# Weight loads and k's block loads issued by GpSimd instead of SyncE, in attention followed by an MLP

## The chip, the cores and the metric

The kernel runs on one core of a Trainium2 chip. The metric is the device time of one execution in microseconds (us); the time before is the median of three runs, 882.17 us (881.49 to 883.12). The core has a matrix engine (TensorE, PE in the profile), three engines for elementwise work (VectorE or DVE, ScalarE or ACT, GpSimd or POOL), and SyncE (SP), which only issues transfers. Each engine works through its own list of instructions in order, and semaphores order them against each other. An engine that reaches an instruction whose semaphore is not there yet stands still, with everything behind it in its list. Transfers between the main memory (HBM) and the on-chip memory (SBUF) run on 16 DMA engines; SP, ACT and POOL can issue them.

## What is computed

The reference has two parts. The first is attention over 4 batches of 8 heads with 768 positions of 64 numbers, in which a query sees only those keys whose hash bucket is equal to its own. The second is an MLP with a learned negative slope on the attention's output.

```python
q_bits = (np.einsum('bhsd,dk->bhsk', q, proj) > 0)      # 6 bits a position; k alike
mask = q_bucket[:, :, :, None] == k_bucket[:, :, None, :]
scores = np.where(mask, scale * np.matmul(q, k.transpose(0, 1, 3, 2)), -1e9)
attn = softmax(scores)                                  # with 1e-9 in the divisor
x = np.matmul(attn, v)  # then (B,H,S,D) -> (B*S, H*D) = 3072 x 512
h = x @ w_in                                            # 512 x 2048
g = np.maximum(h, 0.0) + alpha * np.minimum(h, 0.0)
out = g @ w_out                                         # 2048 x 512
```

q, k, v and proj are float32. The two weight matrices arrive as float64.

## The kernel before

There are two stages. In the first, a loop over 16 pairs of heads does the attention, and beside it the weights are converted. In the second the MLP runs with products of the Strassen kind, so that sums and differences of weight blocks are needed; they are made beside the attention too, and kept in HBM.

The 16 pairs are worked on one after the other (the loop at line 1168). For a pair, PE makes 12 cells of scores (`scores`, lines 760 to 771: two matmuls on hash bits and two on q and k for each cell, into one of three buffers `sc` in PSUM). ACT takes the exponential of each cell into `pt` (L771). PE multiplies with v (`attend`, L801, into `av`). DVE adds the exponentials up (L779 to L790), PE sums these over the partitions (`totals`, L815), and DVE turns and inverts the sums (`divide`, L831 to L834). In the next pair, POOL copies the reciprocals between groups of 32 partitions (L840, L841), DVE spreads them (L843) and multiplies `av` by them (L849), and SP stores the result `x` (L850). The hash bits of the next pair come from PE (L730) and ACT (L736), and POOL's DMAs put them into place (L741, L743): six small transfers a pair, behind ACT's L736.

q and k come in by blocks of 32 x 32 (`load_blocks`, lines 505 to 515): four DMAs for a tensor and pair, each of 32 partitions by 24 runs of 32 numbers. DVE turns the blocks (`turn_blocks`, L704), k's at the start of the pair ahead. ACT takes the largest squares (`magnitude`, L711), after which the buffer is free; there are three buffers for each of q and k, and before the change both are refilled at the end of the pair, for the third pair ahead (lines 1221 to 1224). v has its own load (L488).

The weights come in 32 pieces of 128 x 512 float64 numbers, two a pair (`load_weight`, lines 578 to 582, three buffers `raw`). A piece is converted in steps: ACT reads it (`weight_abs`, L596 and L600), DVE clamps, shifts and joins (L606, L612, L637, L640); L637 is the last to read `raw`, and L640 the last to read ACT's output, which has two buffers. Piece i + 3 is asked for right after the last step of piece i. POOL makes the sums of four pieces (`weight_sums`, L676 and L659), one in front of the reciprocal copies and one before that in most pairs, and SP stores them (L651, L664). From pair 9 on, SP also loads x back and the first weights of the second stage (L864, L880).

The compute instructions are wrapped in `do`, which keeps them in the order of the program. The DMAs are not: a scheduler places them in their engine's list, and each also waits until the DMA eight before it of its kind (those issued by SP and ACT, or those issued by POOL) has landed, since there are eight semaphores for each kind.

Of the kernel before, what the change touches and what calls it, by code (L numbers as in the profile page):

```python
# [407 lines left out]
def fast_path(  # L408
# [12 lines left out]
    nc = tc.nc  # L421
# [33 lines left out]
    NPAIR = len(pairs)  # L455
# [27 lines left out]
    def load(pi, name):  # L483
        b, hp = pairs[pi]
        src = {"q": q, "k": k, "v": v}[name]
        if name == "v":
            t = pool.tile([P, 2, NC * D], F32, name=f"vn{pi}", tag="vn")
            nc.sync.dma_start(t, src[b, 2 * hp : 2 * hp + 2].rearrange("h (p c) d -> p h (c d)", c=NC))  # L488
            nat[name, pi] = t
        elif pi and name in BY_BLOCKS:  # L490
            load_blocks(pi, name)
        else:
            load_part(pi, name, slice(0, NC), nc.sync)

    def load_part(pi, name, cs, queue):
        b, hp = pairs[pi]
        src = {"q": q, "k": k}[name]
        if cs.start == 0:
            nat[name, pi] = pool.tile([P, NC, 2, D], F32, name=f"{name}n{pi}", tag=f"{name}n", bufs=3)
        for s in range(2):  # L500
            queue.dma_start(nat[name, pi][:, cs, s], src[b, 2 * hp + s].rearrange("(p c) d -> p c d", c=NC)[:, cs])

    BY_BLOCKS = 'qk'

    def load_blocks(pi, name):
        b, hp = pairs[pi]
        src = {"q": q, "k": k}[name]
        nat[name, pi] = t = pool.tile([P, NC * 4, 32], F32, name=f"{name}n{pi}", tag=f"{name}n", bufs=3)
        for s in range(2):
            for h in range(2):  # L510
                a = D * s + 32 * h
                nc.sync.dma_start(
                    t[a : a + 32].rearrange("i (c u) d -> i c u d", u=4),
                    src[b, 2 * hp + s, :, 32 * h : 32 * h + 32].rearrange("(u i c) d -> i c u d", u=4, c=NC),
                )
# [39 lines left out]
    raw, wx, wr = {}, {}, {}  # L555
# [3 lines left out]
    def piece(i):  # L559


        if i < HW:
            n, m = divmod(i, 4)
            c, kk = divmod(n, 2)
            o, j = kk + 2 * (m // 2), c + 2 * (m % 2)
            return moe_w_in[o * P : (o + 1) * P, j * 512 : (j + 1) * 512]
        n, m = divmod(i - HW, 2)
        o = n + NI * m
        return moe_w_out[o * P : (o + 1) * P]
# [5 lines left out]
        ahead = (i + 1) * HW // TURNS > HW - len(left[0])  # L575
        order.append(left[0 if left[0] and ahead or not left[1] else 1].pop(0))

    def load_weight(i):
        if i < NW:
            i = order[i]  # L580
            raw[i] = pool.tile([P, 512], moe_w_in.dtype, name=f"raw{i}", tag="raw", bufs=3)
            nc.sync.dma_start(raw[i], piece(i))

    def halves(i):
        words = raw[i].bitcast(U32).rearrange("p (f t) -> p f t", t=2)
# [16 lines left out]
    def weight_clamp(i):  # L602
        if i < NW:
            i = order[i]
            x = wx[i]
            do(DVE.tensor_scalar(x, x, HI_MIN, None, op0=ALU.max, op1=ALU.max, accum_out=wmax[:, i : i + 1]))  # L606
# [76 lines left out]
    def two_banks(name):  # L683
        return psum.tile([P, 2, 512], F32, name=name, tag="sc", bufs=3)
# [17 lines left out]
    def turn_blocks(pi, name):  # L702
        tr[name, pi] = pool.tile([P, S], F32, name=f"{name}T{pi}", tag=f"{name}T")
        do(DVE.transpose(tr[name, pi], nat[name, pi].rearrange("p w d -> p (w d)")))  # L704
# [8 lines left out]
    def hash_bits(pi, halves=BOTH, engine=None):  # L713

        if halves.start == 0:
            bits["q", pi] = qbs[pi % 2]
            kb = pool.tile([P, 3 * CW], BF16, name=f"kb{pi}", tag="kb", bufs=1)
            bits["k", pi] = kb[:, :S]  # L720
            bits["raw", pi] = kb.rearrange("p (a w) -> p a w", w=CW)
        ps = {"k": two_banks(f"hs{pi}")}
        ps["q"] = psum_av.tile([P, 2, 512], F32, name=f"hsq{pi}", tag="av") if engine is DVE else ps["k"]
        for half in range(halves.start, halves.stop):
            for name in "qk" if engine is DVE else "kq":
                for s in range(2):
                    r, c = D * s, D * (s ^ half) + 32 * "kq".index(name)

                    for t, c in [("k", c)] + ([("q", c ^ D)] if engine is DVE and name == "q" else []):
                        do(PE.matmul(  # L730
                            ps[t][c : c + 32, half if t == "k" or engine is not DVE else 0, :CW], wh[r : r + D],
                            tr[name, pi][r : r + D, half * CW : (half + 1) * CW], start=True, stop=True,
                        ))
        if engine is None:
            raw = bits["raw", pi]
            do(ACT.activation(raw[:, 0:3:2], ps["k"][:, :, :CW], AF.Sign, bias=hb))  # L736
            for half in range(2):
                for s in range(2):
                    c = D * (s ^ half)
                    cols = slice(half * CW, (half + 1) * CW)  # L740
                    nc.gpsimd.dma_start(bits["q", pi][D * s : D * s + 32, cols], raw[c + 32 : c + 64, 2 * half])  # L741
                    if half:
                        nc.gpsimd.dma_start(bits["k", pi][D * s : D * s + D, cols], raw[c : c + D, 2])  # L743
            return
        for half in range(halves.start, halves.stop):
            cols = slice(half * CW, (half + 1) * CW)
            for s in range(2):
                c = D * (s ^ half ^ (engine is DVE)) + 32
                do(ACT.activation(
                    bits["q", pi][D * s : D * s + 32, cols], ps["q"][c : c + 32, 0 if engine is DVE else half, :CW], AF.Sign, bias=hb[c : c + 32],  # L750
                ))

            for to, c, n in [(0, 0, P)] if half == 0 else [(0, D, D), (D, 0, D)]:
                dst, src = bits["k", pi][to : to + n, cols], ps["k"][c : c + n, half, :CW]
                do(DVE.tensor_scalar(
                    dst, src, hb_k[c : c + n, 0:1], hb_k[c : c + n, 1:2], op0=ALU.is_gt, op1=ALU.subtract,
                ))
# [19 lines left out]
    def add_first(pi):  # L777
        accp[pi] = pool.tile([P, 2 * NCH, CW], F32, name=f"accp{pi}", tag="accp", bufs=1)
        do(DVE.tensor_tensor(accp[pi], p(0), p(1), op=ALU.add))  # L779
# [362 lines left out]
    for half in (first, second):  # L1142
        turn(0, "q", half)
        turn(0, "k", half, DVE)
        if half is first:
            nil[0]()
            hash_bits(0, first, DVE)
    load(1, "q")
    load(1, "k")
    load_weight(0)  # L1150
    load(0, "v")
    for i in range(1, 3):
        load_weight(i)
# [14 lines left out]
    for pi in range(NPAIR):  # L1168
        i = 2 * pi

        def weight_begin():
            if pi + 1 < NPAIR:
                turn_blocks(pi + 1, "k")
            weight_clamp(i)
            weight_parts(i)
            add_first(pi)

        scores(pi, [c for c in CELLS if pi or c not in ahead])
        if pi:
            divide(pi - 1, weight_begin)  # L1180
        else:
            add_first(pi)
        weight_sum(i)
        weight_group(i)
        load_weight(i + 3)
        if pi == 0:
            weight_abs(1, DVE)
        weight_clamp(i + 1)
        add_third(pi)
        add_last(pi)  # L1190
        add_total(pi)
        weight_parts(i + 1)
        weight_sums(1, weight_sum(i + 1))
        weight_group(i + 1)
        load_weight(i + 4)
        if pi + 1 < NPAIR:
            hash_bits(pi + 1)
            do(ACT.activation(tr["q", pi + 1], tr["q", pi + 1], AF.Copy, scale=DOWN))
        if pi + 2 < NPAIR:
            turn_blocks(pi + 2, "q")  # L1200
        attend(pi)
        if pi + 1 == NPAIR:
            now = ff1(0, 0)
            now.step(1)
        totals(pi)
        if pi + 1 == NPAIR:
            now.step(5)
            divide(pi)
        else:
            weight_abs(i + 2)  # L1210
        if pi + 2 < NPAIR:
            load(pi + 2, "v")
        if pi in (9, 11, 15):
            load_w((9, 11, 15).index(pi))
        if pi in (9, 10, 12):
            load_x(0, *{9: (0,), 10: (2, 3), 12: (1,)}[pi])
        if 11 <= pi < 14 or pi == 15:
            sum_x(0, min(pi - 11, 3), DVE)
        if pi == 1:
            setup_alpha()  # L1220
        for name in "qk":
            magnitude(pi, name)
            if pi + 3 < NPAIR:
                load(pi + 3, name)
        if pi + 1 < NPAIR:
            weight_abs(i + 3)
# [97 lines left out]
```

## Time and profile before

The profile is of one execution. Its own time is 882.06 us; the span, from the first instruction to the last, is 880.2 us.

| | before |
|---|---|
| median of three runs | 882.17 us |
| profiled execution, and its span | 882.06 us, 880.2 us |
| PE busy | 863.0 us (98%) |
| DVE busy | 749.2 us (85%) |
| ACT busy | 368.0 us (42%) |
| POOL busy | 96.8 us (11%) |
| DMAs issued by SP and ACT (queues 1 and 10) | 124.8 MB |
| DMAs issued by POOL (queue 0) | 11.3 MB |
| one pair in the steady state | 19.15 us |
| a k load on SP, of four a pair | 660 ns median to issue, 3.6 us from issue to landing |
| a weight piece on SP | 337 to 364 ns to issue, 4.5 to 4.9 us to landing |
| a bit transfer on POOL (L741) | 505 ns, 3.6 us to landing |
| a 512 KB load on POOL (L989, second stage) | 759 ns, 7.2 us to landing |

How to read it: a row of the groups or the timeline gives engine, line, operation, output tile and input tiles, and in square brackets the idle time before it with what ended it. Rows with a q behind the engine (SPq) are issues of DMAs, whose time is that of issuing and not of moving the data. In the windows, each engine's busy time is followed by the granted PE clock (1.00 is full), the busy share of the DMA engines and GB/s.

### The profile page before, as it was taken

How to read it: one execution, taken by the hardware profiler on the slowest of the kernel's cores; microseconds unless marked ns; L12 is line 12 of the kernel's file. 1: busy time of each engine (PE TensorE's matmuls, PEld its weight loads, DVE VectorE, ACT ScalarE, POOL GpSimd, SP SyncE). 2: the span in 40 equal slices, each digit the busy share in tenths (PEclk: the TensorE clock that was granted, in tenths of full speed). 3: DMA queues.
4: the chain of work that ended last, by engine and by line, in shares of the span. 5: the costliest groups of instructions: out<-in, count | busy, mean ns of one | idle time of the engine just before them, and what ended most of it. 6: DMA issues, size and time to landing. Idle time of an engine off the chain costs nothing.

```text
span 880.2 us, 15210 instructions
## 1 busy us (share of the span) xinstructions
PE 863.0 (98%) x5706; PEld 576.0 (65%) x5706; DVE 749.2 (85%) x1215; ACT 368.0 (42%) x654; POOL 96.8 (11%) x220
## 2 busy tenths in 40 slices
PE   8999999999998999999999999999999999999996
PEld 3444444444443445559996558996557997557996
DVE  5999999999997978899888769898668988668986
ACT  6886888887766752221112222112222112222111
POOL 1221423323322311120000000000000000000000
PEclk9999999999998999999999999999999999999998
DMA  8866797797796347586433425334434333520242
GB/s 197 183 152 136 181 241 157 169 253 192 177 252 169 118 150 263 203 303 223 133 132 90 172 86 197 115 113 125 141 123 155 136 123 96 177 86 1 96 151 69
DMA packets 170819, 137.23 MB, mean 156 GB/s; under 512 B 126016, under 2 KB 154384, under 8 KB 167152
## 3 DMA queue, kind: packets, MB, share of 16 engines
q1 hardware_dynamic: 163136, 123.64, 49.5%
q0 software_dynamic: 5184, 11.34, 3.9%
q10 hardware_dynamic: 2416, 1.18, 0.5%
q8 instruction: 47, 0.77, 0.4%
q14 instruction: 36, 0.29, 0.1%
HBM read 104.87 MB, written 28.31 MB: 151 GB/s over the span
## 4 chain that ended last, share of the span: by engine, by line
PE 92%; DVE 3%; DMA 2%; issue 1%; ACT 1%; SPq 1%; ACTq 0%; DVEq 0%
PE sc L768 15%; PE av L801 13%; PE f_0a L902 2%; PE z_4a L902 2%; PE z_7a L902 2%; PE z_3a L902 2%; PE z_6a L902 2%; PE z_5a L902 2%; PE z_1a L902 2%; PE z_2a L902 2%; PE f_4a L902 2%; PE f_7a L902 2%; PE f_6a L902 2%; PE f_5a L902 2%; PE f_3a L902 2%; PE f_2a L902 2%
## 5 line engine op out<-in xcount | busy, mean ns | idle before, releaser
L771 ACT ACTIVATE pt<-sc 128x768 f32<-128x768 f32 x192 | 154.0, 812 | 8.3 <-PE sc L768 6.8
L768 PE MATMUL sc<-qT,kT 64*128 64x384 f32 x768 | 157.3, 488 | 0.0
L801 PE MATMUL av<-pt,vn 128*32 128x385 f32 (+1 forms) x1536 | 127.4, 486 | 0.0
L801 PEld LDWEIGHTS av<-pt,vn 128*32 128x32 f32 x1536 | 48.7, 109 | 77.5 <-issue 69.3
L768 PEld LDWEIGHTS sc<-qT,kT 64*128 64x128 f32 x768 | 69.3, 190 | 38.4 <-issue 38.1
L768 PE MATMUL sc<-qb,kb 64*128 64x384 bf16 x384 | 63.8, 328 | 8.0 <-ACT pt L771 7.0
L955 DVE TENSOR_TENSOR g<-g,g 128x384 f32<-128x384 f32 x128 | 68.3, 554 | 2.2
L1019 DVE TENSOR_TENSOR gs<-g,gs 128x768 f32<-128x768 f32 x56 | 53.3, 951 | 1.0
L1011 DVE TENSOR_TENSOR ws<-wl 128x512 f32<-128x512 f32 x56 | 38.4, 686 | 18.2 <-DMA wl<-w_out_s 16.3
L1019 DVE TENSOR_TENSOR gs<-g 128x768 f32<-128x768 f32 x56 | 53.2, 951 | 0.0
L596 ACT ACTIVATE wr<-raw 128x512 int32<-128x512 uint32 x32 | 22.1, 692 | 59.1 <-issue 30.2
L741 POOL DMA_DIRECT2D qb<-kb x60 | 30.1, 505 | 146.3 <-ACT kb L736 146.3
L768 PEld LDWEIGHTS <-kb 64*128 64x128 bf16 x384 | 19.6, 95 | 38.7 <-issue 14.1
L779 DVE TENSOR_TENSOR accp<-pt,pt 128x1536 f32<-128x1536 f32 x16 | 28.2, 1760 | 17.9 <-ACT pt L771 17.9
L951 DVE SCALAR_TENSOR_TENSOR g<-h,alpha 128x384 f32<-128x384 f32 x32 | 19.7, 616 | 25.2 <-ACT h L944 25.1
L784 DVE TENSOR_TENSOR accd<-accd,pt 128x1536 f32<-128x1536 f32 x16 | 28.1, 1758 | 1.7
L790 DVE TENSOR_TENSOR accd<-accd,accp 128x1536 f32<-128x1536 f32 x16 | 28.1, 1758 | 0.6
L787 DVE TENSOR_TENSOR accp<-accp,pt 128x1536 f32<-128x1536 f32 x16 | 28.0, 1753 | 0.0
L783 DVE TENSOR_TENSOR accd<-pt,pt 128x1536 f32<-128x1536 f32 x16 | 28.0, 1750 | 0.0
L902 PE MATMUL f_0a<-x,wi 128*128 128x384 f32 x64 | 23.5, 489 | 0.0
L902 PE MATMUL f_1a<-x,wi 128*128 128x384 f32 x64 | 23.3, 486 | 0.0
L902 PE MATMUL f_2a<-x,wi 128*128 128x384 f32 x64 | 23.3, 486 | 0.0
(355 smaller groups left out, 1740.2 us busy)
## 6 DMA issues: line engine op xcount, KB each, us to landing
wi<-w_in_s SPq DMA_DIRECT2D x32, 896.0 KB, 4.7
wl<-w_out_s SPq DMA_DIRECT2D x16, 1024.0 KB, 4.8
wl<-w_out_r SPq DMA_DIRECT2D x12, 1024.0 KB, 5.0
raw<-in_moe_w_out_dram SPq DMA_DIRECT2D x16, 512.0 KB, 4.9
raw<-in_moe_w_in_dram SPq DMA_DIRECT2D x16, 512.0 KB, 4.5
w_in_s<-wsi SPq DMA_DIRECT2D x16, 448.0 KB, 5.7
qn<-in_q_dram SPq DMA_DIRECT2D x64, 96.0 KB, 5.4
vn<-in_v_dram SPq DMA_DIRECT2D x16, 384.0 KB, 5.6
```

The lines of the kernel that those rows point to most:

```text
L741: nc.gpsimd.dma_start(bits["q", pi][D * s : D * s + 32, cols], raw[c + 32 : c + 64, 2 * half])
L768: do(PE.matmul(sc[:, s, :CW], what["k", pi][r, ks], what["q", pi][r, qs], start=first, stop=not first,))
L771: do(ACT.activation(pts[kc][:, g, :, :CW], sc[:, :, :CW], AF.Exp, scale=SCALE / DOWN))
L779: do(DVE.tensor_tensor(accp[pi], p(0), p(1), op=ALU.add))
L783: do(DVE.tensor_tensor(accd[pi], p(3), p(4), op=ALU.add))
L784: do(DVE.tensor_tensor(accd[pi], accd[pi], p(5), op=ALU.add))
L790: do(DVE.tensor_tensor(accd[pi], accd[pi], accp[pi], op=ALU.add))
L801: do(PE.matmul(av[pi][D * s + t : D * s + t + 32, g, :w], nat["v", pi][:, s, kc * D + t : kc * D + t + 32], pts[kc][:, g, s, :w], start=(k ...
L902: do(PE.matmul(self.ps[bank], self.left(left, k), self.right(right, k), start=start and k == 0, stop=k == self.nk - 1, skip_group_check=no ...
L955: do(DVE.tensor_tensor(new_g(b, to)[:, i], g_m[b, x][:, i], g_m[b, y][:, i], op=ALU.subtract))
L1011: do(DVE.tensor_tensor(t, w2[b, n, x], w2[b, n, y], op=op))
L1019: do(DVE.tensor_tensor(t, g2[b, n, x], g2[b, n, y], op=ALU.subtract))
```

## The change

Three things are moved; nothing that is computed is altered.

- `load_weight` issues its DMA on POOL instead of SP. Piece 0 stays on SP and is asked for ahead of q and k of pair 1, instead of behind them.
- `load_blocks` issues k's four DMAs on POOL for pairs 3 and up. q stays on SP.
- From pair 3 on, k is asked for one pair later: in the program no longer at the end of pair pi for pair pi + 3, but inside pair pi, after `divide(pi - 1)`, for pair pi + 2.

In the lists of instructions that the scheduler makes, PE's, DVE's and ACT's compute instructions stand in the same order as before. POOL's list gets 83 more DMAs (52 of k, 31 of the weights). In a steady pair it reads: piece i + 4; the sum of pieces with its small copy; three of k's four DMAs; the copy that waits for `vs` and, where due, another sum; the four reciprocal copies; k's fourth DMA; piece i + 3 of the next turn; the six bit transfers. So three of the four k loads stand ahead of the reciprocal copies and one behind them, while in the program all four come behind. Pieces 1 and 2 come first of all DMAs in POOL's list, behind the memsets of lines 545 and 547.

```diff
     def load_blocks(pi, name):
+        queue = nc.gpsimd if name == "k" and pi > 2 else nc.sync
...
-                nc.sync.dma_start(
+                queue.dma_start(
...
-    def load_weight(i):
+    def load_weight(i, queue=nc.gpsimd):
         if i < NW:
             i = order[i]
             raw[i] = pool.tile([P, 512], moe_w_in.dtype, name=f"raw{i}", tag="raw", bufs=3)
-            nc.sync.dma_start(raw[i], piece(i))
+            queue.dma_start(raw[i], piece(i))
...
+    load_weight(0, nc.sync)
     load(1, "q")
     load(1, "k")
-    load_weight(0)
     load(0, "v")
     for i in range(1, 3):
         load_weight(i)
...
         if pi:
             divide(pi - 1, weight_begin)
+            if pi + 2 < NPAIR:
+                load(pi + 2, "k")
...
             magnitude(pi, name)
-            if pi + 3 < NPAIR:
+            if pi + 3 < NPAIR and name == "q":
                 load(pi + 3, name)
```

## The prediction

> **What bounds the kernel now.** I read the page first: its busy shares, the slices, the chain. TensorE (PE) is busy for 98% of the span, so an edit of loads can only win where PE stands still, and loses where it makes PE stand.
>
> ```profile
> PE 863.0 (98%) x5706; PEld 576.0 (65%) x5706; DVE 749.2 (85%) x1215; ACT 368.0 (42%) x654; POOL 96.8 (11%) x220
> ```
>
> Then PE's own waits, which name almost all of what it waits for in mid-program, two waits on the exponentials:
>
> ```profile
> PE sc L768 <- ACT pt L771: 7.0, 2, 4.3
> ```
>
> The timeline of PE and ACT puts them at 16.65 (2.68 us) and at 269.11 (4.28 us). Both times ACT stood, in order, in front of a conversion of a weight piece that had not landed. First ACT at the start, then ACT, PE and SP near 260:
>
> ```profile
> 15.23 0.67 ACT L596 ACTIVATE wr<-raw 128x512 int32<-128x512 uint32 x1 [2.68 <-DMA raw<-in_moe_w_out_dram]
> 267.15 0.66 ACT L596 ACTIVATE wr<-raw 128x512 int32<-128x512 uint32 x1 [9.10 <-DMA raw<-in_moe_w_out_dram]
> 269.11 0.51 PE L768 MATMUL sc<-qb,kb 64*128 64x384 bf16 x2 [4.28 <-ACT pt L771]
> 269.38 1.51 PE L768 MATMUL sc<-qT,kT 64*128 64x384 f32 x4
> ```
>
> ```profile
> 247.39 6.25 SPq L512 DMA_DIRECT2D kn<-in_k_dram  x4
> 253.74 4.23 SPq L664 DMA_DIRECT2D w_in_s<-wsi  x4
> 258.07 1.80 SPq L850 DMA_DIRECT2D x_s<-x  x1
> 259.96 2.85 SPq L582 DMA_DIRECT2D raw<-in_moe_w_out_dram  x2
> ```
>
> Read the last four: the piece's buffer is free when DVE's L637, which starts at 250.71 and takes 0.68, has read the old piece, at 251.4. SP was busy with k's loads, stores and x until 259.96, 8.6 us later. PE also pays after the gap: in the windows, the granted clock is 1.00 before 264 and
>
> ```profile
> 269.00:274.50 5.50, 5.39 (x22) 3.14 (x23) 2.65 (x2) 3.39 (x6) 0.00 (x0) 0.51 0.92 129
> ```
>
> **What the Trainium skill says.** "TensorE: Matmul & The Clock Gate", What's actually happening: after an idle window of about 3.4 us the array runs at half clock. The trace agrees: 4.28 us idle, then 0.51. "DMA: Bandwidth & Descriptors", Issuing engines are not separate DMA queues: another issuer saves only sequencer time, the same 16 engines move the data. Here sequencer time is what was lost. "Perfetto Trace Analysis", DMA Instruction — SWDGE (GPSIMD): a GpSimd DMA's row ends when the last descriptor is written; so I take the row as POOL's occupation, and four L989 issues in 3.04 us agree. "SBUF — State Buffer", Who interferes with whom: GpSimd's writing of descriptors and a DVE instruction in a 2-port mode block one another. No row of before shows such an overlap.
>
> **Part 1, the stall near 260.** A piece issued by POOL no longer waits behind SP's 12.6 us of other issues. POOL is free there: its reciprocal copies of this pair end at 246.1. Issue at about 251.4, plus the longest landing seen for a piece, 7.1 us, gives 258.5. (The skill's fit in "DMA: Bandwidth & Descriptors", Anatomy of one DMA, is 2.0 us + bytes/436e3, for 512 KB an estimate of 3.2 us without contention; the trace's median is 4.5 to 4.9.) ACT may start L596 when DVE's L640, at 260.82 for 0.69, frees its buffer: 261.5. So 3 us of margin. PE's fourth cell would follow the third (263.85) by 0.81, at 264.66 instead of 269.11: 4.45 us. The four cells from 269.11 take 5.80 us up to 274.91 instead of 4 x 0.81 = 3.24: 2.56 us. Gain **7.0 us**. The DVE waits of 0.84 and 0.18 (st L831, behind the sums of x) stay.
>
> **Part 2, the start.** Piece 0 moves on SP ahead of q1 and k1: issued at 5.1, not 10.73. It is there when ACT is free for it at 12.55, so ACT could win 2.68 us. But pieces 1 and 2 now go out on POOL as soon as its memsets end, at 2.9. Three pieces of 512 KB are 1.57 MB before k1's blocks are through. The windows give the price:
>
> ```profile
> 4.00:14.00 10.00, 9.53 (x74) 4.57 (x74) 4.12 (x6) 5.81 (x10) 0.00 (x0) 1.00 0.82 153
> 14.00:20.00 6.00, 3.35 (x26) 2.18 (x27) 5.15 (x8) 4.77 (x7) 0.00 (x0) 1.00 1.01 341
> ```
>
> At 341 GB/s they take 4.6 us; the engines had 10 x 0.18 = 1.8 us to spare from 4 to 14; so k1 is about 2.8 us later than the 14.17 at which DVE turned it. The same jam may hold q0's second half (PE waits 0.3 us for it already). DVE has 0.49 us in hand before L779 at 17.34 and works without a gap from there to st L831, which ends at 31.79; PE's third cell of pair 1, whose bank st frees, starts at 32.58, 0.79 later. So 2.8 - 0.49 - 0.79 = 1.5 us lost, with PE's head start at ACT worth nothing, since DVE sets the pace. Lower bound: the mix overlaps freely, k1 is 0.7 us later (one issue of 0.66), and PE gains about 0.6 us. Upper bound: 4.6 - 1.28 = 3.3 us lost. I take **1.0 us lost**.
>
> **Part 3, k's loads on POOL.** POOL's rows: a 32-row bit copy takes 501 ns, a 64-row one 521, an L989 load of 512 runs 753. That is 0.525 ns a run; a k load has 32 x 24 = 768 runs of 128 B, so 0.50 + 736 x 0.525 ns = 0.89 us, four a pair, and about 0.55 for each of two pieces (128 rows): 4.7 us on an engine busy for 3.8 to 6.8 of 19.15 us. What matters is the order. In the scheduled program three of k's four loads stand ahead of the reciprocal copies, between the piece's sums and vs; one behind. In the tightest pairs (two L659 sums around vs; five of them) the copies end at 150.26, and DVE wants them at 152.03, both read off one pair's rows (113.73 + 2 x 19.15 for the DVE one):
>
> ```profile
> 145.89 1.28 POOL L659 TENSOR_TENSOR wsi<-wsi 128x512 f32<-128x512 f32 x1
> 147.73 0.18 POOL L676 COPY late_sum<-vs 128x1 f32<-128x1 f32 x1 [0.56 <-DVE vs L836]
> 150.07 0.19 POOL L841 COPY rr<-rr 32x12 f32<-32x12 f32 x1
> 113.73 0.97 DVE L843 STREAM_TRANSPOSE dn<-rr 128x768 f32<-128x768 f32 x1
> ```
>
> Three loads add 2.67, of which POOL's 0.56 wait for vs hides a part: 2.1 us against 1.77 of slack, 0.3 late. Behind L843 on DVE stand L849 and the sums up to st; st has about 0.6 us in hand before PE's third cell (ends 147.02, cell at 147.62). So nothing reaches PE, until the port adds: L612 (0.43 us where L606 on the same tile takes 0.64, so perhaps such a mode) falls into k's issues and can be held by one, 0.9 us, of which DVE's 0.82 wait before L779 takes most. I charge **0.5 us**; from 0 to 3 (five pairs at 0.6). The waits the pieces bring to POOL (for L637) have only the bit copies behind them, which ACT's kb releases later anyway (138.86 against L637's end at 135.5). The bit copies are queued behind a piece and must land within 4.5 us of the last issue (141.46 to 145.99); the median is 3.1, the maximum 5.1, and pieces preceded them by as much before. Nothing charged; if they slip, it is at most a us in the two or three pairs with w_in_s stores. k is used a pair after its load, some 14 us of cover. SP loses four k issues and two pieces a pair: x and v go out earlier, hidden behind PE.
>
> **The sum.** Against the profiled execution's 882.06 us (span 880.2 plus 1.9 around it), which is 0.11 below the median 882.17: -7.0 + 1.0 + 0.5 = -5.5, so 876.6; on the median's footing **876.7 us**.
>
> **Rivals.** *GpSimd becomes the bound*: if a k load takes more than the line through 32 to 512 rows says, the copies of the five tight pairs are late by 3c - 0.56 - 1.77, less 0.6 of cover. At c = 2 us that is 3.1 each, 15 in all: 892 us. It turns the sign from c = 1.4 us. For it: no row of before has 768 short runs on POOL. Against it: three points lie on one line. Chance 0.13. *The piece is late anyway*: near 260 the DMA share is 0.95 to 1.00, so the data and not the issue could be late; then 7.0 falls away and about 883.5 is left. Against it: the piece landed 7.1 us after its issue even there, and has 10. Chance 0.12. *The start wins too*, on free overlap: 875.1, inside the first case. The forecast, with that, has 0.75.
>
> Changes within 0.2% (1.8 us) are about what a measurement of this kernel can't tell from none. The first case alone runs from 873 (start wins 0.6, POOL free, a little of the DVE waits gone) to 880 (start 3.3, POOL 1). The range takes in the late piece and the beginning of GpSimd's case, to 884. Faster: 0.75 and a little of GpSimd's case, 0.76; same: most of the late piece, 0.09; slower 0.15.
>
> **What would show it** (lines of the kernel before). L596 without a DMA wait near 260 and at 15; PE's waits without the 4.28, clock 1.00 throughout 264 to 280; k rows on POOL near 0.9 us; dn L843 waiting under 0.5 us for rr. In pair 1, DVE's kT near 17 and a PE wait on st. I am wrong if k rows take 1.4 us or more, if dn waits for rr by us in many pairs, or if raw still ends a wait of ACT.

## The result and the profile after

The changed kernel takes **889.96 us** (median of four runs, 889.55 to 890.49), against 882.33 us for the kernel before beside it (881.49 to 883.12): the ratio is 1.0086, with a 95% interval from 1.0071 to 1.0100. It is 0.9% slower, 13 us above the forecast of 876.7 and 6 us above the upper end of the range. The profiled execution is 889.55 us, its span 887.8 us. Lines of the changed kernel are one higher than before from L506 on, and three higher behind the main loop's edit.

The page's shares hardly move for PE. POOL is busy for 172.0 us instead of 96.8, and DVE for 9 us more with the same instructions (5.7 us of it at L613):

```profile
PE 866.0 (98%) x5706; PEld 575.8 (65%) x5706; DVE 758.1 (85%) x1215; ACT 365.7 (41%) x654; POOL 172.0 (19%) x303
```

The view of the waits (engine, tile and line, what it waited for: sum in us, number, longest) tells more. PE's two waits on the exponentials, 7.0 us before, are gone. In their place PE waits for DVE, at the sums and their transposes, and once for q. DVE waits ten times for POOL's reciprocal copies, which it hardly did before:

```profile
PE sc L769 <- DVE st L832: 6.7, 8, 2.1
PE sm L816 <- DVE accd L791: 3.0, 4, 1.1
PE tp_q L696 <- DMA qn<-in_q_dram: 2.8, 1, 2.8
...
DVE dn L844 <- POOL rr L842: 9.4, 10, 2.1
```

To place the difference I use the start of the first matmul with v in each pair (L801 before, L802 after, from PE's timeline). It splits the span in three: up to the second pair's first one, the 14 stretches from there to the last pair's, and the rest.

| | second pair | 14 stretches | rest | of the 14: pair 12 to 13 |
|---|---|---|---|---|
| before | 41.56 | 275.78 | 562.84 | 26.52 |
| after | 44.77 | 280.14 | 562.85 | 19.49 |

The rest is the same. The start lost 3.2 us. The 14 stretches lost 4.4 us in all, although the stretch with the old stall won 7.03 us: so 11.4 us were lost in the others. The steady stretch was 19.15 us; eight stretches of the changed kernel are longer than they were, by 0.29 to 2.25 us.

**The stall near 260** went as forecast. ACT's rows of the timeline have no wait for a piece any more. The conversion that stood 9.10 us for its piece is the 28th of 32; it now waits 3.57 us, and for DVE's L641, which frees its output buffer. PE goes on meanwhile, and the granted clock is 1.00 in the windows from 244 to 280 us:

```profile
273.99 0.68 ACT L597 ACTIVATE wr<-raw 128x512 int32<-128x512 uint32 x1 [3.57 <-DVE wsi L641]
```

**The start.** POOL issues two pieces as soon as its memsets end, and PE then stands until q's second half is there; afterwards it runs at about half clock up to about 16 us (1.49 us for a cell's four matmuls that take 0.81 later). From these transposes of q to the third cell PE takes 5.93 us (10.64 to 16.57), against 3.30 in the kernel before (7.19 to 10.49): 2.6 us go to the clock. The last line is that of the windows (from and to; busy time and count of PE, PEld, DVE, ACT, POOL; granted clock, DMA share, GB/s): all DMA engines are busy from 4 to 14 us:

```profile
2.81 0.69 POOL L583 DMA_DIRECT2D raw<-in_moe_w_in_dram  x1
3.50 0.55 POOL L583 DMA_DIRECT2D raw<-in_moe_w_out_dram  x1
...
10.64 0.87 PE L696 MATMUL tp_q<-ident,qn 128*128 128x128 f32 x3 [2.80 <-DMA qn<-in_q_dram]
...
12.38 1.49 PE L769 MATMUL sc<-qT,kT 64*128 64x384 f32 x4
...
4.00:14.00 10.00, 7.16 (x38) 3.68 (x43) 1.79 (x3) 2.41 (x6) 0.05 (x1) 0.77 1.01 233
```

**Late pairs.** First one pair in both kernels: before the change, POOL and then DVE. The second sum ends at 110.85, the copies at 111.97, and DVE's L779, a sum of two inputs, starts at 112.06, 0.09 us later:

```profile
109.57 1.28 POOL L659 TENSOR_TENSOR wsi<-wsi 128x512 f32<-128x512 f32 x1
...
111.78 0.19 POOL L841 COPY rr<-rr 32x12 f32<-32x12 f32 x1
...
110.80 0.43 DVE L612 TENSOR_SCALAR wx<-wx 128x512 uint32<-128x512 uint32 x1
112.06 1.76 DVE L779 TENSOR_TENSOR accp<-pt,pt 128x1536 f32<-128x1536 f32 x1 [0.83 <-ACT pt L771]
```

After, with three k loads ahead:

```profile
114.23 2.58 POOL L513 DMA_DIRECT2D kn<-in_k_dram  x3 [0.48 <-ACT pt L772]
...
116.53 1.68 POOL L660 TENSOR_TENSOR wsi<-wsi 128x512 f32<-128x512 f32 x1
118.27 0.28 POOL L841 COPY rr<-rr 32x12 f32<-32x12 f32 x1
118.59 1.63 POOL L842 COPY rr<-rr 32x12 f32<-32x12 f32 x1
...
115.64 2.87 DVE L613 TENSOR_SCALAR wx<-wx 128x512 uint32<-128x512 uint32 x1
118.43 1.75 DVE L780 TENSOR_TENSOR accp<-pt,pt 128x1536 f32<-128x1536 f32 x1
120.72 0.98 DVE L844 STREAM_TRANSPOSE dn<-rr 128x768 f32<-128x768 f32 x1 [0.55 <-POOL rr L842]
```

L613 takes 2.87 us instead of 0.43 and ends at 118.51, 0.3 us after POOL's second sum. A copy of 12 numbers a partition takes 1.63 us instead of 0.19 and ends at 120.22, just after L780. So the two engines stand in each other's way, first POOL in DVE's and then DVE in POOL's. `dn` starts 6.67 us after `vs` (L837, at 114.05), where it was 4.53 before (109.20 to 113.73): 2.1 us lost in this pair.

L613 is held this long only here. In two other pairs (near 96 and 157 us) the second sum starts just ahead of L780; then L780 waits, and takes 2.50 or 2.67 us instead of 1.76, and the first copy waits for L780 in its turn. In two more (near 177 and 237 us) L780 is 0.07 or 0.08 us ahead, and the second sum takes 2.79 us instead of 1.27; `dn` then waits 2.10 us for the copies. A pair of each kind:

```profile
95.75 1.26 POOL L660 TENSOR_TENSOR wsi<-wsi 128x512 f32<-128x512 f32 x1
96.12 2.50 DVE L780 TENSOR_TENSOR accp<-pt,pt 128x1536 f32<-128x1536 f32 x1 [0.37 <-ACT pt L772]
97.07 1.61 POOL L841 COPY rr<-rr 32x12 f32<-32x12 f32 x1
...
177.37 2.79 POOL L660 TENSOR_TENSOR wsi<-wsi 128x512 f32<-128x512 f32 x1
```

The k loads themselves are what they were taken to be, 0.94 us each (forecast 0.89):

```profile
L513 POOL DMA_DIRECT2D kn<-in_k_dram x52 | 44.5, 944 | 4.4 <-ACT wx L601 2.9
```

### The profile page after: what moved, and what is told of

Read it like the earlier page. It is cut to its first block, busy times and chain, and to the rows that moved or that the text cites. A ratio compares the mean times of both kernels' runs of the same rounds, so it can differ in the third digit from the quotient of the medians.

```text
span 887.8 us, 15216 instructions
## 1 busy us (share of the span) xinstructions
PE 866.0 (98%) x5706; PEld 575.8 (65%) x5706; DVE 758.1 (85%) x1215; ACT 365.7 (41%) x654; POOL 172.0 (19%) x303
## 4 chain that ended last, share of the span: by engine, by line
PE 73%; DVE 12%; POOL 6%; issue 5%; ACT 2%; DMA 1%; ACTq 0%; DVEq 0%; POOLq 0%
PE sc L769 6%; PE av L802 4%; PE f_0a L903 2%; PE z_4a L903 2%; PE z_7a L903 2%; PE z_3a L903 2%; PE z_6a L903 2%; PE z_5a L903 2%; PE z_2a L903 2%; PE z_1a L903 2%; PE f_4a L903 2%; PE f_7a L903 2%; PE f_6a L903 2%; PE f_5a L903 2%; PE f_3a L903 2%
## 5 line engine op out<-in xcount | busy, mean ns | idle before, releaser
L802 PE MATMUL av<-pt,vn 128*32 128x385 f32 (+1 forms) x1536 | 127.4, 486 | 0.1
L802 PEld LDWEIGHTS av<-pt,vn 128*32 128x32 f32 x1536 | 48.9, 109 | 77.5 <-issue 68.0
L513 POOL DMA_DIRECT2D kn<-in_k_dram x52 | 44.5, 944 | 4.4 <-ACT wx L601 2.9
L780 DVE TENSOR_TENSOR accp<-pt,pt 128x1536 f32<-128x1536 f32 x16 | 29.7, 1856 | 4.9 <-ACT pt L772 4.9
L784 DVE TENSOR_TENSOR accd<-pt,pt 128x1536 f32<-128x1536 f32 x16 | 28.0, 1751 | 0.0
L844 DVE STREAM_TRANSPOSE dn<-rr 128x768 f32<-128x768 f32 x16 | 15.6, 976 | 9.5 <-POOL rr L842 9.4
L660 POOL TENSOR_TENSOR wsi<-wsi 128x512 f32<-128x512 f32 x16 | 23.7, 1482 | 0.0
```

What stands on the lines that cost most here:

```text
L513: queue.dma_start(t[a : a + 32].rearrange("i (c u) d -> i c u d", u=4), src[b, 2 * hp + s, :, 32 * h : 32 * h + 32].rearrange("(u i c) d - ...
L802: do(PE.matmul(av[pi][D * s + t : D * s + t + 32, g, :w], nat["v", pi][:, s, kc * D + t : kc * D + t + 32], pts[kc][:, g, s, :w], start=(k ...
```

## The experiments

The theory at the outset: the k loads ahead of the reciprocal copies push POOL's second sum and the copies into DVE's L613 and L780, with which they share a port (about 11 us); pieces 1 and 2 on POOL make the start late (3 us); moving the later pieces wins 7 us. The rivals: writing k's descriptors disturbs DVE wherever it stands; the bit transfers or pieces are late on POOL's queue; it takes k and the pieces together.

All results, with the split of each profiled span as above. Times are medians, each beside runs of the kernel before on the same chip. There were three chips: e1 to e4, e5 to e8 and e9 to e11 share one each, and the medians of the kernel before were 882.12, 881.98 and 882.24 us there.

| kernel | us | ratio to before, 95% | second pair | 14 stretches |
|---|---|---|---|---|
| e1_weights | 877.38 | 0.9953 [0.9937, 0.9969] | 41.99 | 270.32 |
| e2_k_behind | 878.95 | 0.9967 [0.9954, 0.9980] | 43.74 | 270.27 |
| e3_start | 884.36 | 1.0027 [1.0015, 1.0038] | 44.40 | 274.83 |
| e4_k_only | 884.92 | 1.0037 [1.0023, 1.0051] | 43.67 | 276.30 |
| e5_delay | 895.66 | 1.0159 [1.0136, 1.0182] | 45.64 | 285.09 |
| e6_piece0 | 877.05 | 0.9939 [0.9920, 0.9959] | 41.56 | 270.46 |
| e7_k_and_piece0 | 877.18 | 0.9941 [0.9921, 0.9960] | 42.21 | 270.23 |
| e8_two_ahead | 884.27 | 1.0022 [1.0013, 1.0030] | 44.14 | 274.07 |
| e9_sum_x | 875.98 | 0.9933 [0.9917, 0.9950] | 41.64 | 269.07 |
| e10_sum_last | 880.79 | 0.9984 [0.9977, 0.9992] | 45.38 | 271.58 |
| e11_both | 875.69 | 0.9930 [0.9913, 0.9946] | 41.01 | 269.15 |

The column of the second pair varies from one execution to the next: e4 has the list of issues of before at its start, and its profiled execution reaches the second pair 2.1 us later. Two cells at half clock are 1.5 us of this, behind a wait of 2.39 us, while in the profile of before a wait of 2.68 us is followed by cells of 0.82 us:

```profile
17.28 0.50 PE L769 MATMUL sc<-qb,kb 64*128 64x384 bf16 x2 [2.39 <-ACT pt L772]
17.55 1.51 PE L769 MATMUL sc<-qT,kT 64*128 64x384 f32 x4
```

So I read the start from medians, and the 14 stretches from the profiles. The medians don't free it of this either: e4's is 2.8 us above before, and its stretches explain 0.5. A start that costs some 2 us therefore needs more than one comparison.

### The change in its parts: e1, e2, e3, e4

**e1_weights**: the pieces alone.

```diff
     def load_weight(i):
         if i < NW:
+            queue = nc.gpsimd if i > 2 else nc.sync
...
-            nc.sync.dma_start(raw[i], piece(i))
+            queue.dma_start(raw[i], piece(i))
```

> The kernel before, with one part of the change: weight pieces 3 to 31 are issued by GpSimd. The start (pieces 0 to 2) and all of k's loads stay on SyncE. Theory: the wait of 9.1 us near 260 was SyncE's queue alone, so it goes and nothing else comes: 882.3 - 7.0 = 875.3 us, the period of pair 12 to 13 falls from 26.52 to about 19.5 us, and all other pairs keep 19.15. Rival (the pieces themselves disturb GpSimd: the bit transfers queued behind a piece that waits for its buffer are late, or descriptors hold VectorE): 878 to 883 us, with PE waits on sc or on the bits in several pairs.

Measured: 877.38 us, 4.7 below before, not 7.0. The stretch from pair 12 to 13 fell from 26.52 to 19.50 us, as expected, and twelve of the others stay within 0.05 us. But the stretch from 13 to 14 rose from 19.14 to 20.60 us. There DVE's sum of two blocks of x (L875) meets POOL's sum, takes 1.61 us instead of the 0.92 that it took a pair earlier, and holds up `st`, for which PE waits; and a reciprocal copy is held by L780. POOL, DVE, PE and POOL again, from the timeline of e1_weights:

```profile
282.27 1.27 POOL L660 TENSOR_TENSOR wsi<-wsi 128x512 f32<-128x512 f32 x1
...
282.76 1.61 DVE L875 TENSOR_TENSOR x<-x,x 128x768 f32<-128x768 f32 x1
...
284.98 0.34 PE L769 MATMUL sc<-qb,kb 64*128 64x384 bf16 x2 [1.28 <-DVE st L832]
...
287.74 1.79 POOL L841 COPY rr<-rr 32x12 f32<-32x12 f32 x1
```

Before, DVE had caught up during the stall (busy for 2.65 of the 5.5 us from 269). So 1.5 us of the 7.0 come back one pair later; the remaining 0.8 us is the start (0.4 later in this execution) and the second stage (0.4 longer), where nothing was changed. The rival is out: no pair waits for a bit or a piece.

**e2_k_behind**: the changed kernel with k's DMAs held in program order, so that all four stand behind the copies.

```diff
-                queue.dma_start(
+                pinned(queue is nc.gpsimd, queue.dma_start(
```

> The changed kernel, with all four k loads of a pair issued behind the reciprocal copies instead of three ahead and one behind. Number, size and issuing engine of every transfer are those of the changed kernel. Theory (three loads ahead push the sum L660 and the copies L841/L842 about 2 us later, into VectorE's L613 and two-input L780, where they share a port): the copies take 0.19 us again, dn no longer waits for rr, and the 11.4 us of late pairs go: 890.0 - 11.4 = 878.6 us, with the 3.2 us of the start still in it. Rival 1 (writing k's 3072 descriptors a pair on GpSimd holds VectorE wherever it stands): 886 to 890 us. Rival 2 (the bit transfers and pieces on GpSimd's queue are late behind k): 888 to 895 us, with the four loads now in one piece ahead of them.

Measured: 878.95 us. The 14 stretches take 270.27 us, those of e1 to 0.05 us. In the pair shown above the copies take 0.19 us again, and k's four loads follow them (of the 64 in the run two are still held, as in e1):

```profile
113.98 0.19 POOL L842 COPY rr<-rr 32x12 f32<-32x12 f32 x1
115.00 3.43 POOL L513 DMA_DIRECT2D kn<-in_k_dram  x4 [0.83 <-ACT pt L772]
```

The same 52 loads on the same engine cost 11.0 us where they stand in the change (9.9 in the 14 stretches; the rest lies at the start, where both have one list), and nothing behind the copies. Both rivals are out. Descriptor writing does hold DVE a little: L613 is longer than 0.5 us three times here (0.53 to 0.78), always until 0.25 us after the end of the k load that it met, 0.7 us in all, and PE sees none of it.

**e3_start**: piece 0 on SP ahead of q and k of pair 1, pieces 1 and 2 on POOL, all else as before.

```diff
+            queue = nc.gpsimd if i in (1, 2) else nc.sync
...
+    load_weight(0)
     load(1, "q")
     load(1, "k")
-    load_weight(0)
```

> The kernel before, with the start of the change alone: piece 0 on SyncE ahead of q and k of pair 1, pieces 1 and 2 on GpSimd; everything later as before. Theory (q0's second half lands late behind three pieces, PE waits 2.8 us for it and then runs at half clock): +3.2 us, 885.5 us, the first matmul with v at 25.6 us instead of 22.4, and the wait near 260 untouched. Rival (the start's loss is made good later, since ACT no longer waits 2.7 us for piece 0): 882 to 883 us.

Measured: 884.36 us, 2.2 above before, with q's second half as the first thing late. PE starts on it at 11.14 us, 3.95 later than before (7.19):

```profile
11.14 0.52 PE L696 MATMUL tp_q<-ident,qn 128*128 128x128 f32 x3 [4.23 <-DMA qn<-in_q_dram]
```

The second pair comes 2.84 us later. That is these 3.95 us and 1.6 us of half clock behind them (4.88 us from here to the third cell, against 3.30), less 2.7 us, as ACT's wait for piece 0 is gone. The stall shrank by 1.4 us, which takes back a part.

One trace could be chance, given how starts vary, but the 13 divide without overlap: in the six kernels with pieces 1 and 2 on POOL, PE starts on q's second half at 10.49 to 11.40 us, in the seven others at 7.09 to 7.66.

**e4_k_only**: k on POOL as in the change; all weights' loads and the start as before.

```diff
-    def load_weight(i, queue=nc.gpsimd):
+    def load_weight(i, queue=nc.sync):
...
-    load_weight(0, nc.sync)
     load(1, "q")
     load(1, "k")
+    load_weight(0)
```

> The kernel before, with k's part of the change alone: k's loads of pairs 3 and up on GpSimd, asked for one pair later, three ahead of the reciprocal copies; all weight pieces and the start as before. Theory (the three loads ahead make the copies collide with VectorE): late pairs of some 11 us as in the changed kernel; the wait near 260 shrinks or goes too, since SyncE has lost the 6.25 us of k's issues that stood ahead of that piece: 882.3 + 11 - 7 = 886 us, up to 893 if the wait stays. Rival (it takes k's loads and the pieces together on GpSimd to make it late): 875 to 878 us.

Measured: 884.92 us. The total is near the 886 expected, but not for the reason expected. The late pairs cost only 2.45 us (0.18 to 0.72 each), and the stall shrank by only 1.95 (26.52 to 24.57): the piece was still issued behind 7.73 us of stores, at 262.31. Why so little lateness? Without pieces in POOL's list one k load goes out in POOL's idle time ahead of the first sum, and only two stand between the sums:

```profile
106.27 0.86 POOL L513 DMA_DIRECT2D kn<-in_k_dram  x1 [0.57 <-ACT kn L712]
...
111.64 1.69 POOL L513 DMA_DIRECT2D kn<-in_k_dram  x2
```

That led to e8.

### Delay or descriptors: e5, e8, e10

**e5_delay**: e2 with memsets instead of k loads in that place.

```diff
+    idle = pool.tile([P, S], BF16, name="idle", bufs=1)
...
+        if 0 < pi < NPAIR - 2:
+            for w in (S, S, S, S, S // 2):
+                do(POOL.memset(idle[:, :w], 0.0))
         weight_sums(1, vsum[pi])
```

One of the five goes out in POOL's idle time ahead of the piece, so 3.5 stand between the sums, as the expectation says.

> The kernel e2_k_behind (all four k loads behind the reciprocal copies), with 3.5 memsets of a tile that nobody reads put on GpSimd between the piece's sum and the copy that waits for vs, in the pairs that load k; they take about 2.6 us together, as the three k loads do there, and write no descriptors. Theory (it is the delay of the second sum and of the copies, which then meet VectorE's L613 and L780): as late as the changed kernel, 878.95 + 11 = 890 us, copies of up to 1.8 us, dn waiting for rr in most pairs. Rival (it is the writing of descriptors beside VectorE): the copies are late but short, which costs what the prediction's slack leaves uncovered, at most 0.6 us in the pairs with a second sum: 879 to 882 us.

Measured: 895.66 us, 16.7 above e2_k_behind, more than the changed kernel. No descriptor is written there. The timeline of DVE and POOL, by start:

```profile
114.73 0.87 DVE L834 TENSOR_SCALAR rc<-st 128x12 f32<-128x12 f32 x1
...
114.84 2.80 POOL L841 MEMSET idle<- 128x768 bf16 x4
...
117.84 1.74 DVE L781 TENSOR_TENSOR accp<-pt,pt 128x1536 f32<-128x1536 f32 x1
...
117.91 2.81 POOL L660 TENSOR_TENSOR wsi<-wsi 128x512 f32<-128x512 f32 x1
...
121.70 0.98 DVE L848 STREAM_TRANSPOSE dn<-rr 128x768 f32<-128x768 f32 x1 [2.12 <-POOL rr L846]
```

POOL's sum starts 0.07 us after DVE's L781, stands until that ends at 119.58, and then takes 1.1 us more; DVE waits 2.12 us for the copies. But the run is not as clean as I wanted. PE waits twice, 3.0 us in all, for bit transfers, which now stand behind k's four loads and a piece. And the memsets hold DVE too: L834, of 0.17 us, stands 0.87 us in the line above, until the first memset ends, and over nine pairs its excess is 4.2 us. Taking both off the 14.8 us by which the 14 stretches exceed e2's leaves 7.6 us for the delay alone, an estimate, since it takes DVE's excess as lost to PE in full. That speaks for the theory, which had 11, and against 3 at most; e8 and e10 ask the same without memsets.

**e8_two_ahead**: the changed kernel with two k loads ahead of the copies and two behind (`load_blocks` gets the halves as an argument).

```diff
+            if pi + 2 < NPAIR:
+                load_blocks(pi + 2, "k", 0)
             divide(pi - 1, weight_begin)
             if pi + 2 < NPAIR:
-                load(pi + 2, "k")
+                load_blocks(pi + 2, "k", 1)
```

> The changed kernel with two of k's four loads ahead of the reciprocal copies and two behind, instead of three and one. Theory (there is a threshold: VectorE wants the copies 1.75 us after they are made, and GpSimd's 0.5 us wait for vs hides as much; two loads of about 0.85 us stay near it, three go over it): 1 to 4 us above e2_k_behind, 880 to 883 us, as the k loads alone cost some 2.5 us in e4_k_only, where two stood ahead. Rival (every load ahead costs the same): 878.95 + 2/3 x 11.0 = 886.3 us.

Measured: 884.27 us, 5.3 above e2_k_behind, between what the theory (1 to 4) and the rival (7.3) gave, nearer the theory's end. The 14 stretches, which leave the start out, settle it better: 270.27 us with no load ahead, 274.07 with two, 280.14 with three. The first two cost 1.9 us each, the third 6.1. It isn't the same for every load, but neither is there the free allowance that I had thought of: DVE and POOL block one another already with two. L615 starts while a k load is issued and, before that lets it go, the sum has begun; it ends 0.3 us after the sum.

```profile
112.77 1.73 POOL L515 DMA_DIRECT2D kn<-in_k_dram  x2 [0.47 <-ACT pt L774]
...
114.38 1.53 POOL L662 TENSOR_TENSOR wsi<-wsi 128x512 f32<-128x512 f32 x1
...
116.29 1.63 POOL L844 COPY rr<-rr 32x12 f32<-32x12 f32 x1
...
114.19 2.01 DVE L615 TENSOR_SCALAR wx<-wx 128x512 uint32<-128x512 uint32 x1
```

**e10_sum_last**: e8 with the second sum behind the copies; as many loads ahead.

```diff
-        weight_sums(1, vsum[pi])
         for q0 in (0, D):
...
+        weight_sums(1, vsum[pi])
         between()
```

> The kernel e8_two_ahead (two k loads ahead of the reciprocal copies) with the copy that waits for vs and GpSimd's second sum moved behind the four reciprocal copies; as many k loads stand ahead of the copies as before. Theory (the loss comes where a GpSimd instruction that reads SBUF meets VectorE's L615 or L782 on the shared port, and copies that are done before L782 lose nothing): copies of 0.19 us, L615 at 0.43 us; the second sum now meets L782 instead and costs part of it: 880 to 882 us, against 884.3 for e8_two_ahead. Rival (what counts is how much issuing stands ahead of the copies): 884 us, as e8_two_ahead.

Measured: 880.79 us, 3.5 below e8_two_ahead, with the same issuing ahead of the copies; the 14 stretches fall by 2.5 us. In the pair shown for e8, L615 takes 0.57 us. Of 64 reciprocal copies two are held for over 1 us, against nine in e8:

```profile
115.67 0.57 DVE L615 TENSOR_SCALAR wx<-wx 128x512 uint32<-128x512 uint32 x1
...
116.54 1.67 POOL L842 COPY rr<-rr 32x12 f32<-32x12 f32 x1
```

The rival, which counts the issuing ahead of the copies, is out. But with the sum gone from in front of them the copies also come some 1.5 us sooner, so e10 by itself doesn't part the meeting of two instructions from the plain length of POOL's list ahead of the copies. Two of its pairs do (near 97 and 155 us): the copies end 0.3 us ahead of L782, `dn` waits for nothing, but the sum starts 0.1 us ahead of L782, which takes 2.78 us instead of 1.75, and the two stretches that follow are still 0.5 us longer than 19.15.

Over the traces of before, after, e1, e2, e4, e5 and e8 I took every reciprocal copy longer than 1 us. There are none before, eight after and 31 in all. Each of the 31 lies in the same DVE line (L779 of the kernel before) and ends 0.05 or 0.06 us after it. In the six other traces there are nine more, all alike. So a copy that is late only by the length of POOL's list doesn't take longer; one that starts while this line runs does.

### The start and the place where the gain went: e6, e7, e9, e11

**e6_piece0**: e1 with `load_weight(0)` ahead of q and k of pair 1 on SP; pieces 1 and 2 stay behind v on SP.

```diff
+    load_weight(0)
     load(1, "q")
     load(1, "k")
-    load_weight(0)
```

> The kernel e1_weights with piece 0 asked for ahead of q and k of pair 1, as in the change, and pieces 1 and 2 left on SyncE behind v. Theory (pieces 1 and 2 on GpSimd made the start late, piece 0 did not): q0's second half is not late, ACT no longer waits 3.1 us for piece 0, but VectorE, which turns k of pair 1 some 1.5 us later, sets the pace: 876.5 to 877.5 us, against 877.4 for e1_weights. Rival 1 (one early piece is enough to hold q0's second half or k): 878 to 879.5 us. Rival 2 (PE keeps ACT's 3.1 us): 874 to 875 us.

Measured: 877.05 us, as the theory has it. ACT's wait for piece 0 is gone and the first matmul with v starts at 19.66, 3.2 us sooner than in e1; then PE waits for DVE twice and has lost nearly all of it by the second pair (41.56 against 41.99):

```profile
29.36 0.86 PE L816 MATMUL sm<-accd,ones 128*32 128x192 f32 x16 [1.73 <-DVE accd L791]
...
32.58 0.34 PE L769 MATMUL sc<-qb,kb 64*128 64x384 bf16 x2 [0.64 <-DVE st L832]
```

**e7_k_and_piece0**: the changed kernel with both repairs, `pinned` as in e2 and in `load_weight`:

```diff
+            queue = nc.gpsimd if i > 2 else nc.sync
```

> The changed kernel with two repairs: all four k loads of a pair behind the reciprocal copies, as in e2_k_behind, and pieces 1 and 2 at the start on SyncE behind v, as in e6_piece0. Theory (k behind the copies costs nothing, and the rest of e2's 878.95 is the start): equal to e6_piece0 within 0.7 us. Rival (52 k loads on GpSimd cost something wherever they stand): 1 to 3 us above e6_piece0.

Measured: 877.18 us, 0.13 above e6. So k on POOL behind the copies costs nothing and wins nothing, and the start of the change costs 1.8 us here (878.95 less 877.18), 2.2 by itself in e3.

**e9_sum_x**: e6 with three of DVE's sums of x moved from ahead of `st` to behind L850 of the next pair.

```diff
             divide(pi - 1, weight_begin)
+            if 12 <= pi < 15:
+                sum_x(0, pi - 12, DVE)
...
-        if 11 <= pi < 14 or pi == 15:
-            sum_x(0, min(pi - 11, 3), DVE)
+        if pi == 15:
+            sum_x(0, 3, DVE)
```

> The kernel e6_piece0 with VectorE's three sums of x (L875) of pairs 11 to 13 moved from ahead of st to behind L850 of the next pair. Theory (once the wait near 260 is gone, these sums come ahead of st, the longest held at 1.61 us by GpSimd's sum, and make PE wait; that took back some 1.5 us of the 7.0 in the pair 13 to 14, which takes 20.60 us): that pair falls to about 19.2 to 19.5 us: 877.05 - 1.4 = 875.6 us, 874.5 to 876. Rival (VectorE has no room there wherever the sums stand): 876.7 to 877.4 us.

Measured: 875.98 us, 1.07 below e6, at the upper edge of what was expected. The stretch from 13 to 14 falls from 20.60 only to 19.91 us, as DVE is still behind there and PE waits 0.54 us for `st`; from 11 to 12, which was not in the expectation, it falls from 20.19 to 19.15; and 0.6 us comes back in the last stretch. So the sums ahead of `st` are part of what came after the stall, not the whole.

**e11_both**: e9 with e10's order on POOL.

> The kernel e9_sum_x with the second sum behind the reciprocal copies as in e10_sum_last; k stays on SyncE. Theory (without k ahead the sum and the copies end just before L780 as they are, so the move has little to win, and the sum may now meet L780): within 1 us of e9_sum_x outside pairs 12 to 14, where copies of 1.7 us go: 874 to 877 us. Rival (the copies were already in the way in every pair): 2 us or more below e9_sum_x.

Measured: 875.69 us, within the error of e9. No copy is held any more, and the time is the same: with the copies done 0.09 us before L780 in the steady pairs, the conflict costs nothing there. e9 and e11 are the fastest here, 0.7% below before. That the weights' loads alone (e1) give 0.5% of it is the useful part of the change.

## Why the prediction was wrong

The change in its parts is -4.7 us for the pieces (e1), +1.8 for the start (e2 less e7) and +11.0 for k (changed kernel less e2): some 8 us, against 7.6 measured. The prediction had -7.0, +1.0 and +0.5.

**Part 1, the stall: right at its place, too large in the end.** The sum had 7.0 us, from 26.52 to 19.50 or 19.49 measured: 7.03. The sentence that failed is "the DVE waits of 0.84 and 0.18 (st L831, behind the sums of x) stay". Without the stall the larger one became 1.28 us, and the stretch from 13 to 14 grew by 1.5. I had asked where the stall goes, but not who had used it to catch up. e1 gave 4.7 us in place of 7.0.

**Part 2, the start: the mechanism was half named, and the term was too small.** I took 1.0 us lost, with an upper bound of 3.3; it was 2.2 in e3 and 3.2 in the profile of the changed kernel. I priced it through k of pair 1 and DVE's slack of 0.49 and 0.79 us. What was late first was q's second half, which I had mentioned and not priced: 3.95 us in e3. The clock behind it I put at nothing without a reason, and it cost 1.6 us in e3 and 2.6 in the changed kernel. The idle window of about 3.4 us that the prediction quotes is no safe limit: half clock followed waits of 2.80 us (changed kernel) and 2.39 us (e4), and not the one of 2.68 us in the kernel before. Here the measurement decides: the length of a wait doesn't tell by itself. I had priced the jam at the 341 GB/s seen from 14 to 20 us before; with all DMA engines busy, 233 GB/s were moved from 4 to 14 us, at which two pieces take 4.5 us and not 3.1. The part on piece 0 held: "PE's head start at ACT worth nothing, since DVE sets the pace" is what e6 shows.

**Part 3, k on POOL: the mechanism was missed, 0.5 us forecast, 11.0 measured** (changed kernel less e2). The issue time was right (0.94 us against 0.89), so my rival "GpSimd becomes the bound", which needed 1.4 us or more, was not what happened, though its sign was right. The step that failed is "2.1 us against 1.77 of slack, 0.3 late". The 1.77 us between the end of the copies and `dn` is L779's own length (1.76). I read it as time in which the copies could run, but while L779 runs they can't: the 31 held copies all end with it. The room was the 0.09 us before L779 starts. Behind this lies the second miss: I let the second sum move 2 us without asking what it would meet. It met L612 (L613 after), to which I gave at most 0.9 us, and that for descriptors; it was held for up to 2.4 us, by a k load and then by the sum behind it. And it met L779 (L780 after), where either held the other. Eight stretches became longer, not five (a sum stands behind `vs` in eight of the sixteen pairs).

"SBUF — State Buffer" in the Trainium skill, Who interferes with whom, states the rule that I left out beside the one I used: a DVE instruction with two SBUF inputs contends with a GpSimd instruction that reads SBUF, and not with one that only writes; and whichever comes first has the shared pair for its whole instruction, the other waits. The traces agree, with 1.63 us for a copy of 0.19 beside L780, 2.79 for the sum of 1.27 behind L780 and 2.50 for L780 behind the sum; and beside POOL's issues of DMAs, 29 of DVE's two-input sums (L783, L784) of the kernel before take 1.75 or 1.76 us, like those that are alone. L613 has one input, so this rule isn't about it; the section's other rule, which the prediction quotes, sets a DVE instruction in a 2-port mode against GpSimd's instructions in general, and I took it for descriptors alone. L613's 2.87 us instead of 0.43, up to the end of the sum, would fit that, but no trace shows the mode. I cited the section and looked for one kind of overlap in the trace of before, found none, and stopped; the overlap that matters was one that did not exist yet and that the moved loads made.

The same page's sentence on descriptors also holds here: L613 waits for the k load that it meets (up to 0.78 us in e2): by itself 0.7 us in all, and hidden.

What stays open: how the 9.9 us from the three loads divide. DVE's waits for the copies grew by 8.4 us in all (9.4 against 1.0), L613 is longer by 5.7 and L780 by 1.5; how much of each reaches PE isn't shown, since these overlap with other waits. And it isn't shown what decides on the clock at the start, where executions with one list of issues differ by up to 2 us.

## What to carry to other kernels

Idle time between a producer and its consumer is slack only if the producer's instruction can run in it; when the time is the length of an instruction that holds it off, as L779 does the copies, the slack ends where that instruction begins. When DMAs are moved to an engine that also computes, ask what each compute instruction behind them will meet after the shift, and put the issues behind the work that others wait for: the same 52 loads cost 11 us where three of four stood ahead of four small copies, and nothing behind them. And a stall that is removed was somebody's time to catch up; look for who is late in the pair after it.

## What was unexpected in the hardware

- A POOL copy of 12 numbers a partition (0.19 us) takes 1.3 to 1.8 us when it starts during DVE's two-input sum, and ends 0.05 or 0.06 us after it, 40 times of 40 in the 13 traces.
- Some 0.1 us decides who waits. In e5, POOL's sum starts 0.07 us after DVE's and takes 2.81 us instead of 1.27; in e10 it starts 0.10 us before, and DVE's takes 2.78 us instead of 1.75. In the kernel before the copies end 0.09 us ahead of DVE's sum and nothing is held.
- A memset on POOL holds a DVE instruction on small tiles (L834) to its own end: 0.87 us instead of 0.17, in five pairs of e5.
- Two pieces of 512 KB from POOL's queue at 2.8 and 3.5 us held back q's second half, issued on SP at 3.98, by 3.95 us (e3): with 1.2 and 0.5 us of head start on another engine's queue, the pieces landed at 8.65 and 10.02 us and q's two transfers at 10.52 and 11.00 (6.63 and 7.06 in the kernel before).
- Half clock followed waits of PE of 2.39 us (e4) and 2.80 us (changed kernel), and not one of 2.68 us (kernel before).
